# Pooled attention feeding a GELU MLP: first batch by two head pairs at a time, v over two queues, weight loads in longer runs, one multiply moved ahead of an eviction

## The chip, the cores and the metric

The kernel runs on one core of a Trainium2 chip. The metric is the device time in microseconds (us) of one execution; smaller is better. Five engines work side by side, each with its own list of instructions that it takes in order: TensorE (PE; its weight loads are shown as PEld), VectorE (DVE), ScalarE (ACT), GpSimd (POOL) and SyncE (SP). SP, ACT and POOL also issue DMA transfers, and the profile numbers the queues behind them: q1 belongs to SP, q10 to ACT, q0 to POOL.

## What is computed

q, k and v are f32, 8 batches x 8 heads x 576 positions x 64. k and v are averaged over groups of 8 positions, so that each head has 72 keys. Attention follows, its result is laid out as 4608 rows of 512, and an MLP with a tanh GELU takes it to the output.

```python
k_p = k.reshape(B, H, 72, 8, D).mean(axis=3)
v_p = v.reshape(B, H, 72, 8, D).mean(axis=3)
attn = softmax(scale * q @ k_p^T)            # 8 x 8 x 576 x 72
x = (attn @ v_p).transpose(0, 2, 1, 3).reshape(4608, 512)
out = gelu_tanh(x @ w_in) @ w_out            # 512 -> 2048 -> 512
```

## The kernel before, in words

**Two interleaved pipelines.** Attention goes batch by batch (8 batches of 576 rows), the MLP group by group (`NG` = 9 groups of 512 rows). Attention fills `xT`, the transposed input of the MLP, column by column. While group g is in its second multiplication (`p2_mm`, L290), the attention of batch g+1 is woven into it by hand: `todo` (L397 to L428) says ahead of which of the 64 second-multiplication matmuls each step of the attention stands. The schedule is manual: each engine executes its instructions in the order in which the program writes them down, and waits are put in by the framework where data or buffers ask for it.

**Attention of a batch.** For each of 8 items (c, pr), c being a half of the queries and pr a pair of heads: `qk` (L208) makes two score matmuls into two PSUM banks, `expo` (L216) takes the exponential on ACT, `av` (L224) multiplies with v and with ones (which gives the softmax's denominators), `norm` (L241) takes Ln and Exp(-x) on ACT, which is the reciprocal, and `mult` (L252) multiplies on DVE into `xT`. k and v are pooled by DVE additions (`k_steps` L147, `v_steps` L154). `trans_k` (L168) transposes pooled k on PE and copies it into `kTs`, even rows for c = 0 and odd rows for c = 1; `trans_q` (L184) transposes q in four pieces `QG`, two of queries with heads 0 to 3 and two with heads 4 to 7.

**An MLP group.** `p1_mm` (L280): for each of 16 chunks fo of 128 hidden units, 4 matmuls over ko = 0..3 (128 rows of the input each), 512 columns. `gelu` (L285) evicts the chunk on ACT. Then 4 x 16 matmuls of `p2_mm`, and `store` (L294), a DVE eviction and four output DMAs for each 128 rows. Chunk ko of the first multiplication reads what head pair ko of the attention gave.

**The start, batch 0 (L95 to L140 and L305 to L348).** SP and ACT load k, SP loads v in two halves of four heads; each half comes as two DMAs, partitions 0 to 63 and 64 to 71. POOL loads q in two halves, then, in the order of its queue: the first two quarters of w_in, k and q of batch 1, the other two quarters of w_in, four quarters of w_out. PE runs `spin` matmuls (L309), which nobody reads, to stay busy. All 8 score items come first, then the 8 items' `av`, `norm` and `mult` one after the other. After the fourth `mult`, a small memset of the v buffer (L344) releases SP to load v of batch 1. The first 16 first-multiplication matmuls on the 288 columns of c = 0 are put among the last items; the other 224 columns follow.

**Group 0 (L351 on).** Beside its chunks fo stand, by `plan` (L372), the preparation of batch 1: k additions at fo 0, k transpose at 4, four q transposes at 6 to 9, v additions at 10 and 12. Its second multiplication runs in blocks of four fo over two output banks, so that it starts on the first quarter of w_out alone.

**At each change of group** (L404 to L415), the last item's multiply comes after the 64th matmul, and the seventh item's too (position 55 + 9 = 64), so that DVE takes the last eviction of the group ahead of both. The first matmuls of the next group follow at once on PE; those with ko = 2 and 3 read what the seventh and eighth multiply write.

Of the kernel before, what the change touches and what calls it, by code (L numbers as in the profile page):

```python
# [18 lines left out]
def kernel(  # L19
# [45 lines left out]
    def load_k(b, engs):  # L65
        rows = k[b].rearrange("h (j l) d -> (h j) (l d)", l=8)
        main = rows[0:128 * KR].rearrange("(p r) c -> p r c", r=KR)
        n = KR // len(engs)
        for i, eng in enumerate(engs):
            eng.dma_start(out=kts[b % 2][:, i * n:(i + 1) * n], in_=main[:, i * n:(i + 1) * n])  # L70
        engs[-1].dma_start(out=kts[b % 2][64:128, KR], in_=rows[128 * KR:])

    def load_v(b, eng, h0=0, h1=H):
        if b not in vs:
            vs[b] = kvp.tile([Sp, H, 512], F32, name="vt")
        rows = v[b, h0:h1].rearrange("h (j l) d -> j h (l d)", l=8)

        for j0, j1 in ((0, 64), (64, Sp)) if eng is nc.sync else ((0, Sp),):
            eng.dma_start(out=vs[b][j0:j1, h0:h1], in_=rows[j0:j1])
# [8 lines left out]
    w_in_b = consts.tile([128, KO, DF], BF16, name="w_in_b")  # L88
    w_out_b = consts.tile([128, FO, DM], BF16, name="w_out_b")
    w_in_v = moe_w_in.rearrange("(ko p) f -> p ko f", p=128)  # L90
    w_out_v = moe_w_out.rearrange("(fo p) d -> p fo d", p=128)
# [4 lines left out]
    load_v(0, nc.sync, 0, 4)  # L96
    load_v(0, nc.sync, 4, 8)
# [4 lines left out]
    def load_w_in(i):  # L102
        nc.gpsimd.dma_start(out=w_in_b[:, :, i * 512:(i + 1) * 512], in_=w_in_v[:, :, i * 512:(i + 1) * 512])  # L103

    load_w_in(0)
    load_w_in(1)
# [4 lines left out]
    kTs = [consts.tile([128, 2, H, Sp], BF16, name=f"kT{i}") for i in range(2)]  # L111
# [11 lines left out]
    nc.vector.memset(kTs[0], 0.0)  # L123
# [4 lines left out]
    nc.gpsimd.memset(kTs[1], 0.0)  # L128
    nc.gpsimd.memset(kps[1], 0.0)
    nc.gpsimd.memset(kts[1][0:64, KR], 0.0)  # L130
    nc.gpsimd.memset(vps[0], 8.0)  # L131
    nc.gpsimd.memset(vps[1], 8.0)  # L132

    load_k(1, [nc.gpsimd])
    load_q(1)
    load_w_in(2)
    load_w_in(3)
    for i in range(4):
        nc.gpsimd.dma_start(out=w_out_b[:, 4 * i:4 * i + 4, :], in_=w_out_v[:, 4 * i:4 * i + 4, :])

# [27 lines left out]
    def trans_k(b, bank, odd_eng=None):  # L168
        tp = half_bank(bank)[:, 0:(KR + 1) * 128].rearrange("p (r c) -> p r c", c=128)
        kf = kps[b % 2].rearrange("p r d -> p (r d)")  # L170
        for r in range(KR + 1):
            nc.tensor.transpose(out=tp[:, r, :], in_=kf[:, r * D:r * D + 128], identity=identb)  # L172
        tp = tp[0:D]
        n7 = (H - 1) * KH
        for e in range(2):
            copy = nc.scalar.copy if e and odd_eng is nc.scalar else nc.vector.tensor_copy
            o = kTs[b % 2][e * 64:(e + 1) * 64, e]
            copy(out=o[:, 0:H - 1].rearrange("p h (j r) -> p h j r", r=KR),  # L178
                 in_=tp[:, 0:KR, 0:n7].rearrange("p r (h j) -> p h j r", j=KH))
            copy(out=o[:, H - 1, 0:(128 - n7) * KR].rearrange("p (j r) -> p j r", r=KR),  # L180
                 in_=tp[:, 0:KR, n7:128].rearrange("p r j -> p j r"))
            copy(out=o[:, H - 1, (128 - n7) * KR:], in_=tp[:, KR, 64:128])

    def trans_q(b, i, t0, n, bank, eng):  # L184
        if b not in qTs:
            qTs[b] = bp.tile([128, 2, TP, 128], BF16, name="qT")
        tp = half_bank(bank)[:, 0:n * 128].rearrange("p (t c) -> p t c", c=128)
        for x in range(n):
            nc.tensor.transpose(out=half_bank(bank)[:, x * 128:(x + 1) * 128],
                                in_=qs[b][:, i, (t0 + x) * 128:(t0 + x + 1) * 128],  # L190
                                identity=identb)
        o = qTs[b][:, i, t0:t0 + n]
        if eng is nc.scalar:
            nc.scalar.copy(out=o, in_=tp)
        else:
            nc.vector.tensor_copy(out=o, in_=tp)

# [10 lines left out]
    def qk(b, c, pr, bank):  # L208
        for e in range(2):
            h = 2 * pr + e  # L210
            nc.tensor.matmul(out=PS[:Sp, bank + e, :CH].rearrange("j (t p) -> j t p", p=32),  # L211
                             lhsT=kTs[b % 2][:, c, h, :],
                             rhs=qTs[b][:, h // 4, :, h % 4 * 32:h % 4 * 32 + 32],
                             start=True, stop=True)
# [26 lines left out]
    def norm(b, c, pr, bank):  # L241
        ld = ep.tile([128, CH], F32, name="ld")
        if b:
            nc.scalar.activation(out=ld[0:64], in_=PS[64:128, bank, :CH], func=ACT.Ln)  # L244
            nc.scalar.activation(out=ld[64:128], in_=PS[0:64, bank + 1, :CH], func=ACT.Ln)  # L245
        else:
            nc.scalar.activation(out=ld, in_=PS[:, bank + 1, :CH], func=ACT.Ln)
        rc = ep.tile([128, CH], F32, name="rc")
        nc.scalar.activation(out=rc, in_=ld, func=ACT.Exp, scale=-1.0)  # L249
        rcs[b, c, pr] = rc  # L250

    def mult(b, c, pr, bank):  # L252
        rc = rcs.pop((b, c, pr))
        col = b * S + c * CH
        for x in range(2 if b else 1):
            rows = slice(x * 64, (x + 1) * 64) if b else slice(0, 128)
            nc.vector.tensor_tensor(out=xT[rows, pr, col:col + CH], in0=PS[rows, bank + x, :CH],  # L257
                                    in1=rc[rows], op=ALU.mult)

# [9 lines left out]
    def h_bank(g, fo):  # L269
        x, y = x_bank(g), 1 - x_bank(g)  # L270
        if fo == 4:
            return 7
        return (x, 2, 3, y)[fo if fo < 4 else (fo - 1) % 4]
# [6 lines left out]
    def p1_mm(g, fo, ko, c0=0, c1=GROUP):  # L280
        r0 = g * GROUP
        nc.tensor.matmul(out=PS[:, h_bank(g, fo), c0:c1], lhsT=w_in_b[:, ko, fo * 128:(fo + 1) * 128],  # L282
                         rhs=xT[:, ko, r0 + c0:r0 + c1], start=(ko == 0), stop=(ko == KO - 1))
# [20 lines left out]

    act_set(EXP_SET)  # L305
    for s in k_steps(0):
        s()

    def spin(n):  # L309

        for _ in range(n):
            nc.tensor.matmul(out=PS[:, 7, :], lhsT=idle[:, 0:128], rhs=idle, start=True, stop=True)  # L312

    def scores(b, c, pr, bank):
        qk(b, c, pr, bank)
        expo(b, c, pr, bank)

    spin(16)
    trans_q(0, *QG[0], 5, nc.scalar)
    trans_q(0, *QG[1], 6, nc.scalar)  # L320
    spin(4)
    trans_k(0, 4, nc.scalar)
    trans_q(0, *QG[2], 5, nc.vector)
    trans_q(0, *QG[3], 6, nc.vector)
    spin(2)
    for i, (c, pr) in enumerate(((0, 0), (0, 1), (1, 0), (1, 1), (0, 2), (0, 3), (1, 2), (1, 3))):
        if i:
            spin(1)
        scores(0, c, pr, (2, 0)[i % 2])
    for hf in range(2):  # L330
        for s in v_steps(0, hf):
            s()

    early = [(fo, ko) for ko in range(KO) for fo in range(4)]
    take = (0, 0, 0, 0, 0, 4, 6, 6)
    for i, (c, pr) in enumerate(ORDER):
        bank = (4, 6, 0, 2, 4, 6, 4, 6)[i]
        av(0, c, pr, bank)
        norm(0, c, pr, bank)
        mult(0, c, pr, bank)  # L340
        if i == 3:

            vs[1] = kvp.tile([Sp, H, 512], F32, name="vt")
            nc.vector.memset(vs[1][:, 0, 0:1], 0.0)  # L344
            load_v(1, nc.sync)
        for fo, ko in early[:take[i]]:
            p1_mm(0, fo, ko, 0, CH)
        early = early[take[i]:]  # L348


    for g in range(NG):  # L351
        nb = g + 1 if g + 1 < B else None
        act_set(GELU_SET)
        if g + 2 < B:

            load_q(g + 2)
            trans_q_dma(g + 2)
            nc.gpsimd.tensor_copy(out=gate, in_=qTs[g + 2][0:1, 1, TP - 1, 0:2])  # L358
            load_k(g + 2, [nc.gpsimd])
            load_v(g + 2, nc.gpsimd)  # L360


        side = {fo: [] for fo in range(FO)}
        if nb is not None:
            kk = k_steps(nb)
            v0, v1 = v_steps(nb, 0), v_steps(nb, 1)
            tk = [lambda: trans_k(nb, 4)]
            if g:
                plan = {2: kk[:1], 3: kk[1:], 7: v0[:1], 8: v0[1:], 9: tk, 11: v1[:1], 12: v1[1:]}
            else:  # L370
                tq = [lambda a=a, i=i: trans_q(nb, *a, 4 + i, nc.vector) for i, a in enumerate(QG)]
                plan = {0: kk, 4: tk, 6: tq[:1], 7: tq[1:2], 8: tq[2:3], 9: tq[3:], 10: v0, 12: v1}  # L372
# [5 lines left out]
        if g == 0:  # L378
            first = [(fo, ko, CH) for ko in range(KO) for fo in range(4)]
        else:  # L380
            late = 3
            rest = [fo for fo in range(4) if fo != late]
            first = [(fo, ko, 0) for ko in range(2) for fo in rest]
            first += [(late, 0, 0), (late, 1, 0)]
            first += [(fo, ko, 0) for ko in (2, 3) for fo in rest + [late]]
        for fo, ko, c0 in first:
            p1_mm(g, fo, ko, c0)
        for fo in range(FO):
# [4 lines left out]
            for s in side[fo]:  # L393
                s()

# [6 lines left out]
        if nb is not None:  # L402
            act_set(EXP_SET)
            pos = (6, 14, 20, 27, 34, 41, 48, 55, 61)  # L404
            for i in range(len(ORDER) + 1):
# [7 lines left out]
                if i:  # L413
                    at(pos[i], norm, *a)
                    at(min(pos[i] + 9, 65), mult, *a)  # L415
# [43 lines left out]
```

The softmax here doesn't subtract the row's maximum and nothing guards it: scores larger than these inputs give would overflow.

## Time and profile before

| what | value |
|---|---|
| device time, median of 3 runs | 311.97 us (310.83 to 312.3) |
| device time of the profiled execution | 311.66 us |
| its span, first to last instruction | 309.9 us |
| granted TensorE clock, mean | 0.999 |
| PE busy | 296.7 us (96%) |
| ACT busy | 220.9 us (71%) |
| DVE busy | 157.1 us (51%) |
| L282 and L291, the MLP's matmuls, of 128x512 | 548 and 560 in the trace, 379 ns each |
| weight loads of L282 (128 columns) | 98 ns each |
| read from HBM, written | 36.70 MB, 9.44 MB |

Spans of PE overlap, since matmuls are pipelined: the 379 ns of a matmul are its latency, and a dense run of them starts one about every 216 ns. So 16 of them make a row of 3.63 us in the timeline (15 starts and one latency). Times within the execution are counted from the start of the span. A bracket at the end of a line of the timeline tells how long the engine had been idle and what ended that. In the view of DMAs by stretch, a share is the time that packets of a queue took, as part of 16 engines' time; shares add up to over 100% where packets overlap.

### The profile page before, as it was taken

How to read it: one execution, taken by the hardware profiler on the slowest of the kernel's cores; microseconds unless marked ns; L12 is line 12 of the kernel's file. 1: busy time of each engine (PE TensorE's matmuls, PEld its weight loads, DVE VectorE, ACT ScalarE, POOL GpSimd, SP SyncE). 2: the span in 40 equal slices, each digit the busy share in tenths (PEclk: the TensorE clock that was granted, in tenths of full speed). 3: DMA queues.
4: the chain of work that ended last, by engine and by line, in shares of the span. 5: the costliest groups of instructions: out<-in, count | busy, mean ns of one | idle time of the engine just before them, and what ended most of it. 6: DMA issues, size and time to landing. Idle time of an engine off the chain costs nothing.

```text
span 309.9 us, 4249 instructions
## 1 busy us (share of the span) xinstructions
PE 296.7 (96%) x1516; PEld 149.5 (48%) x1545; DVE 157.1 (51%) x304; ACT 220.9 (71%) x414; POOL 30.8 (10%) x54
## 2 busy tenths in 40 slices
PE   7788899999999999999999999999999999999994
PEld 2455455444544455445544554455445544444441
DVE  3867536647568455855495358636772640020011
ACT  1597478877997799778987898689868987306500
POOL 8530000300301200030003000200000000000000
PEclk9999999999999999999999999999999999999999
DMA  7999995894895982588358826572101120121022
GB/s 225 232 279 249 178 200 116 266 225 87 258 224 113 237 186 62 112 225 175 85 110 232 185 68 100 166 182 68 41 0 33 49 56 0 36 68 34 2 68 69
DMA packets 32701, 41.05 MB, mean 132 GB/s; under 512 B 17608, under 2 KB 21704, under 8 KB 31784
## 3 DMA queue, kind: packets, MB, share of 16 engines
q0 software_dynamic: 10160, 24.26, 35.4%
q1 hardware_dynamic: 22200, 15.74, 21.8%
q10 hardware_dynamic: 320, 0.79, 0.8%
q8 instruction: 12, 0.20, 0.3%
q14 instruction: 9, 0.07, 0.1%
HBM read 36.70 MB, written 9.44 MB: 149 GB/s over the span
## 4 chain that ended last, share of the span: by engine, by line
PE 83%; DMA 12%; POOL 2%; issue 1%; ACT 0%; DVE 0%; POOLq 0%
PE PS L291 38%; PE PS L282 36%; DMA w_out_b<-in_moe_w_out_dram 8%; DMA kt<-in_k_dram 4%; PE PS L211 4%; PE PS L231 4%; PE PS L172 1%; POOL w_in_b L103 0%; POOL kT L128 0%; POOL qb L84 0%; POOL vp L131 0%; POOL vp L132 0%; DVE osb L296 0%; ACT e L218 0%; POOL kt L130 0%
## 5 line engine op out<-in xcount | busy, mean ns | idle before, releaser
L291 PE MATMUL PS<-w_out_b,gT 128*128 128x512 bf16 x560 | 133.8, 379 | 0.9
L282 PE MATMUL PS<-xT,w_in_b 128*128 128x512 bf16 (+2 forms) x580 | 128.3, 373 | 1.8 <-DMA w_in_b<-in_moe_w_in_dram 0.9
L288 ACT ACTIVATE gT<-PS 128x512 bf16<-128x512 f32 x144 | 81.3, 603 | 48.4 <-PE PS L282 48.2
L282 PEld LDWEIGHTS <-w_in_b 128*128 128x128 bf16 x592 | 57.2, 98 | 66.4 <-issue 2.0
L291 PEld LDWEIGHTS <-gT 128*128 128x128 bf16 x576 | 56.0, 97 | 57.1 <-issue 0.8
L296 DVE COPY osb<-PS 128x512 f32<-128x512 f32 x36 | 24.9, 692 | 94.9 <-PE PS L291 94.9
L257 DVE TENSOR_TENSOR xT<-PS,rc 64x288 bf16<-64x288 f32 (+1 forms) x120 | 54.6, 455 | 29.9 <-ACT rc L249 22.3
L218 ACT ACTIVATE e<-PS 72x576 bf16<-72x576 f32 x64 | 40.7, 644 | 8.4 <-PE PS L211 7.6
L145 DVE TENSOR_TENSOR vt<-vt 72x1024 f32<-72x1024 f32 (+1 forms) x32 | 30.5, 952 | 7.0 <-DMA vt<-in_v_dram 6.2
L249 ACT ACTIVATE rc<-ld 128x288 f32<-128x288 f32 x64 | 28.3, 443 | 2.1
L211 PE MATMUL PS<-qT,kT 128*72 128x288 bf16 x128 | 26.1, 286 | 0.4 <-ACT e L218 0.3
L244 ACT ACTIVATE ld<-PS 64x288 f32<-64x288 f32 x56 | 22.8, 408 | 1.4
L245 ACT ACTIVATE ld<-PS 64x288 f32<-64x288 f32 x56 | 22.5, 402 | 1.4
L263 ACT ACT_TABLE_LOAD x17 | 21.8, 1283 | 2.1 <-issue 1.8
L231 PE MATMUL PS<-e,vp 72*128 72x288 bf16 x112 | 23.1, 285 | 0.0
L211 PEld LDWEIGHTS <-kT 128*72 128x72 bf16 x128 | 14.4, 113 | 14.2 <-issue 1.4
L145 DVE TENSOR_TENSOR kt<-kt 128x1280 f32<-128x1280 f32 (+1 forms) x16 | 18.5, 1158 | 4.7 <-DMA kt<-in_k_dram 4.3
L358 POOL COPY gate<-qT 1x2 bf16<-1x2 bf16 x6 | 1.1, 176 | 155.8 <-DMA qT<-qb 155.8
L178 DVE COPY kT<-PS 64x504 bf16<-64x504 bf16 x15 | 10.1, 675 | 7.1 <-PE PS L172 7.0
L231 PEld LDWEIGHTS <-vp 72*128 72x128 bf16 x112 | 11.0, 98 | 3.3
L312 PE MATMUL PS<-idle 128*128 128x512 bf16 x28 | 9.6, 467 | 1.2 <-DVE idle L120 1.2
L145 DVE TENSOR_TENSOR vp<-vt 72x128 bf16<-72x128 f32 x28 | 6.9, 284 | 0.6
(45 smaller groups left out, 75.5 us busy)
## 6 DMA issues: line engine op xcount, KB each, us to landing
out_dram<-osb SPq DMA_DIRECT2D x142, 64.0 KB, 1.7
kt<-in_k_dram POOLq DMA_DIRECT2D x7, 1024.0 KB, 5.8
vt<-in_v_dram POOLq DMA_DIRECT2D x6, 1152.0 KB, 12.4
qb<-in_q_dram POOLq DMA_DIRECT2D x7, 576.0 KB, 15.1
w_in_b<-in_moe_w_in_dram POOLq DMA_DIRECT2D x4, 512.0 KB, 18.4
w_out_b<-in_moe_w_out_dram POOLq DMA_DIRECT2D x4, 512.0 KB, 25.0
vt<-in_v_dram SPq DMA_DIRECT2D x2, 512.0 KB, 11.1
vt<-in_v_dram SPq DMA_DIRECT2D x1, 1024.0 KB, 11.6
```

What stands on the lines that cost most here:

```text
L145: nc.vector.tensor_tensor(out=o, in0=a, in1=b, op=ALU.add)
L211: nc.tensor.matmul(out=PS[:Sp, bank + e, :CH].rearrange("j (t p) -> j t p", p=32), lhsT=kTs[b % 2][:, c, h, :], rhs=qTs[b][:, h // 4, :, h ...
L218: nc.scalar.activation(out=e, in_=PS[:Sp, bank:bank + 2, :CH], func=ACT.Exp, scale=1.0 / 64.0)
L231: nc.tensor.matmul(out=PS[:, bank + x, :CH], lhsT=flat(vps[b % 2][:, pr, x]), rhs=e[:, x, :], start=True, stop=True)
L244: nc.scalar.activation(out=ld[0:64], in_=PS[64:128, bank, :CH], func=ACT.Ln)
L245: nc.scalar.activation(out=ld[64:128], in_=PS[0:64, bank + 1, :CH], func=ACT.Ln)
L249: nc.scalar.activation(out=rc, in_=ld, func=ACT.Exp, scale=-1.0)
L257: nc.vector.tensor_tensor(out=xT[rows, pr, col:col + CH], in0=PS[rows, bank + x, :CH], in1=rc[rows], op=ALU.mult)
L282: nc.tensor.matmul(out=PS[:, h_bank(g, fo), c0:c1], lhsT=w_in_b[:, ko, fo * 128:(fo + 1) * 128], rhs=xT[:, ko, r0 + c0:r0 + c1], start=(ko ...
L288: nc.scalar.activation(out=gTs[g][:, fo, :], in_=PS[:, h_bank(g, fo), :], func=ACT.Gelu_apprx_tanh)
L291: nc.tensor.matmul(out=PS[:, o_bank(g, r), :], lhsT=gTs[g][:, fo, r * 128:(r + 1) * 128], rhs=w_out_b[:, fo, :], start=(fo == 0), stop=(fo ...
L296: nc.vector.tensor_copy(out=osb, in_=PS[:, o_bank(g, r), :])
```

## The change

- **Loads.** v of batch 0: the first half on SP, the second on ACT, no longer both on SP. The last piece of k moves from ACT to SP. w_in comes as two halves of 1024 columns (4 KB runs of f32) in two tiles, no longer four quarters (2 KB runs). w_out's rows are dealt to partitions in fours, so that each of its four DMAs reads 8 KB runs. For that the hidden units of a chunk are taken with a step of four: the weight load of `p1_mm` reads every fourth column. POOL's queue is now q (two), first half of w_in, k of batch 1 (ahead of most of its memsets), second half of w_in, q of batch 1, w_out.
- **Batch 0.** Pooled k first in the transposes; all copies of transposed k on DVE. The first v addition stands on DVE ahead of the two copies of transposed q for heads 4 to 7. `av`, `norm` and `mult` go by two head pairs: one Ln, one Exp and one multiply of 128 x 2 x 288. The order is pairs 0 and 1 for c = 0, then c = 1, then pairs 2 and 3. The last three DVE additions of v's second half stand after the first multiply. Spins fill the waits (22 at the start, then 6, 5, 2 and 3); they write into banks of the attention, so they wait for the multiplies that read those.
- **Group 0's first 16 matmuls** are of 512 columns into banks 4 to 7, after the last spins. v of batch 1 is released by the memset after the third (of four) multiplies.
- **Plan of group 0.** k transposes at fo 6, q transposes at 10 to 13, v additions at 13 and 14. Loads for batch 2 are written after the chunks, not ahead of them.
- **Every batch.** `kTs` is two tiles; the seventh multiply stands at position 62 at the latest, ahead of the last eviction, no longer after it.

```diff
-        engs[-1].dma_start(out=kts[b % 2][64:128, KR], in_=rows[128 * KR:])
+        engs[0].dma_start(out=kts[b % 2][64:128, KR], in_=rows[128 * KR:])
...
+    HALVES = [((0, 64, h, h + 4), (64, Sp, h, h + 4)) for h in (0, 4)]
+    WHOLE = ((0, 64, 0, H), (64, Sp, 0, H))
...
-    w_out_v = moe_w_out.rearrange("(fo p) d -> p fo d", p=128)
+    w_out_v = moe_w_out.rearrange("(q p j) d -> p q (j d)", p=128, j=4)
...
-    load_v(0, nc.sync, 0, 4)
-    load_v(0, nc.sync, 4, 8)
+    load_v(0, nc.sync, HALVES[0])
+    load_v(0, nc.scalar, HALVES[1])
...
-        nc.gpsimd.dma_start(out=w_in_b[:, :, i * 512:(i + 1) * 512], in_=w_in_v[:, :, i * 512:(i + 1) * 512])
+        nc.gpsimd.dma_start(out=w_in_b[i], in_=w_in_v[:, :, i * 1024:(i + 1) * 1024])
...
+    def norm0(c, pr, bank):
+        ld = ep.tile([128, 2, CH], F32, name="ld0", bufs=1)
+        nc.scalar.activation(out=ld, in_=PS[:, bank + 1:bank + 4:2, :CH], func=ACT.Ln)
+        rc = ep.tile([128, 2, CH], F32, name="rc0")
+        nc.scalar.activation(out=rc, in_=ld, func=ACT.Exp, scale=-1.0)
+        nc.vector.tensor_tensor(out=xT[:, pr:pr + 2, c * CH:(c + 1) * CH], in0=PS[:, bank:bank + 3:2, :CH],
+                                in1=rc, op=ALU.mult)
...
-        nc.tensor.matmul(out=PS[:, h_bank(g, fo), c0:c1], lhsT=w_in_b[:, ko, fo * 128:(fo + 1) * 128],
+        q, j = divmod(fo % 8, 4)
+        nc.tensor.matmul(out=PS[:, h_bank(g, fo), c0:c1], lhsT=w_in_b[fo // 8][:, ko, q * 512 + j:(q + 1) * 512:4],
...
+    spin(22, 1)
+    t = kts[0]
+    for r in (slice(0, KR), slice(KR, KR + 1)):
+        add(t[:, r, 0:256], t[:, r, 0:256], t[:, r, 256:512])
+    for s in k_steps(0)[1:]:
+        s()
+    nc.gpsimd.memset(kps[1], 0.0)
+    nc.gpsimd.memset(kts[1][0:64, KR], 0.0)
+    load_k(1, [nc.gpsimd])
+    load_w_in(1)
+    load_q(1)
...
+    trans_k(0, 4)
+    trans_q(0, *QG[0], 5, nc.scalar)
+    trans_q(0, *QG[1], 6, nc.scalar)
+    scores(0, 0, 2)
+    scores(0, 1, 0)
+    va[0]()
+    trans_q(0, *QG[2], 5, nc.vector)
+    trans_q(0, *QG[3], 6, nc.vector)
+    for i, (c, pr) in enumerate(((1, 0), (1, 1), (0, 2), (0, 3), (1, 2), (1, 3))):
+        spin(1, 7)
+        scores(c, pr, (2, 0)[i % 2])
+    for s in va[1:] + vb[:1]:
+        s()
...
+    early = [(fo, ko) for ko in range(2) for fo in range(4)]
+    av0(0, 0, 4)
+    norm0(0, 0, 4)
+    for s in vb[1:]:
+        s()
+    av0(1, 0, 0)
+    norm0(1, 0, 0)
+    spin(5, 5)
+    av0(0, 2, 4)
+    norm0(0, 2, 4)
+    vs[1] = kvp.tile([Sp, H, 512], F32, name="vt")
+    nc.vector.memset(vs[1][:, 0, 0:1], 0.0)
+    load_v(1, nc.sync, WHOLE)
+    spin(2, 1)
+    av0(1, 2, 0)
+    norm0(1, 2, 0)
+    spin(3, 5)
+    for fo, ko in early:
+        p1_mm(0, fo, ko)
...
-                plan = {0: kk, 4: tk, 6: tq[:1], 7: tq[1:2], 8: tq[2:3], 9: tq[3:], 10: v0, 12: v1}
+                plan = {0: kk, 6: tk, 10: tq[:1], 11: tq[1:2], 12: tq[2:3], 13: tq[3:] + v0, 14: v1}
...
-                    at(min(pos[i] + 9, 65), mult, *a)
+                    at(min(pos[i] + 9, 62 if i < len(ORDER) else 65), mult, *a)
```

## The prediction

> **What bounds the kernel now.** I read the page's slices first, then a table of busy time by stage, then the timeline of the first 60 us.
>
> ```profile
> PE   7788899999999999999999999999999999999994
> PEclk9999999999999999999999999999999999999999
> ```
>
> ```profile
> 0.00:12.46 12.46, 8.47 (x45) 3.86 (x46) 6.35 (x15) 3.21 (x6) 11.07 (x21) 1.00 0.89 233
> 12.46:16.67 4.21, 3.94 (x24) 2.45 (x24) 2.87 (x7) 3.76 (x7) 0.05 (x1) 1.00 1.38 201
> 16.67:25.65 8.98, 7.90 (x66) 6.03 (x64) 6.60 (x14) 8.17 (x19) 2.92 (x4) 1.00 1.13 277
> 25.65:40.03 14.38, 12.29 (x72) 5.92 (x72) 9.69 (x20) 8.52 (x15) 0.00 (x0) 1.00 1.28 211
> 40.03:58.33 18.30, 18.05 (x96) 9.58 (x97) 7.95 (x17) 15.95 (x32) 2.94 (x5) 1.00 0.83 163
> 58.33:90.45 32.12, 31.94 (x164) 16.11 (x166) 19.34 (x37) 26.62 (x51) 2.92 (x5) 1.00 0.81 215
> ```
>
> After each stretch stand its length, the busy time of PE, PEld, DVE, ACT and POOL, the granted clock, the DMA share and GB/s. From 58.33 on PE is full (31.94 of 32.12 us) at the full clock, and the change adds no PE work there. So it is decided ahead of 58.33, where group 0's second multiplication ends. From the first score matmul (12.46) to there are 45.87 us; the work in it, at one start per 0.216 us for 512 columns, 0.122 for 288 and 0.056 for 128, is 128 x 0.216 + 80 x 0.122 + 23 x 0.056 = 38.7. These 7 us of waits and spins, and part of the 12.46, are all there is to win. Up to 40 us the DMA engines are full too (shares of about 1).
>
> **Part 1: to the first scores.** k's additions start at 7.25, with its last piece. Split, its main part (in by 6.4) goes first: 1024 elements 1.22 us (the 72x1024 row), 256 elements about 0.42 (on the line through 0.69 for 512 and 1.22 for 1024), then 0.83 and 0.49. Pooled k is ready at 9.4, not 10.13. The scores also wait for ACT's two copies of transposed q (0.69 and 0.59): they start at 11.55 and the exponentials at 12.0, **0.9 earlier**.
>
> **Part 2: v over two queues.** How queues share is in the DMA view from 6.5 to 10 us:
>
> ```profile
> q0 software_dynamic: 237, 0.47, 70.0%
> q1 hardware_dynamic: 235, 0.46, 38.6%
> ```
>
> Packets, MB, share. The two take turns packet by packet (237 to 235), though one of q takes 0.165 us (70% of 16 x 3.5 us, by 237) and one of v 0.092. With three queues a turn is 2 x 0.092 + 0.165 = 0.35 us, 46 packets per us and queue. When k's main part is through (landed at 6.0, so 5.3 or a little earlier), SP has k's last 64 packets and 288 of v ahead of it: 7.7 us, and about 1 us to land: v's first half is in at **14.0**. Before, DVE took it at 12.82 without waiting for it. The second half, on ACT, comes at about 13 and not at 16.5:
>
> ```profile
> 12.82 1.93 DVE L145 TENSOR_TENSOR vt<-vt 72x1024 f32<-72x1024 f32 x2
> ...
> 16.54 1.94 DVE L145 TENSOR_TENSOR vt<-vt 72x1024 f32<-72x1024 f32 x2 [1.27 <-DMA vt<-in_v_dram]
> 18.52 0.49 DVE L145 TENSOR_TENSOR vz<-vt 72x128 bf16<-72x128 f32 x2
> ```
>
> Bounds for the first half: 11.7, if k, q and v alone fill the engines (256 x 0.149 + 640 x 0.092 + 256 x 0.165 = 139, 8.7 us by 16, from 2 us on and 1 us to land; 0.149 is half the 0.298 of part 4), and 14.6, if the 8-partition piece goes slowly at the end. I take 14.0.
>
> Behind that addition stand, on DVE, the copies of transposed q for heads 4 to 7; for them waits the fifth score item, and on PE, in order, everything after it. Addition 1.22, copies 0.49 and 0.42: 16.2. The fifth exponential starts 0.45 later (as 12.46 to 12.91 before), at 16.65; four at 0.575 end at 19.0. Before, the eight ended at 17.5. So part 1's gain becomes a **loss of 1.5**.
>
> **Part 3: norm by two pairs.** ACT: Ln of 288 takes 0.395, Exp 0.443; with 0.93 ns per further element (0.395 to GELU's 0.603 at 512) 576 take 0.66 and 0.71, less 0.06 overlap: 1.3 per two pairs, where two single ones took 1.55 (0.775 apart). That saves 1.0 in all. But fewer, longer links chain PE, ACT and DVE: av of two pairs 8 x 0.122 = 0.98 (18.0 to 19.0), 0.2 lag, 1.3 on ACT (20.5), multiply 0.76 (21.3; 0.455 for 288 plus 288 x 1.04 ns), then v's second half 0.69 + 0.49 (22.5), for which the third av waits; 0.98, 0.2, 1.3 and 0.8 more end the third multiply at 25.9. The spins after it wait for its banks: 3 x 0.216, and the first MLP matmul starts at **26.5**. The fourth multiply is done at 27.2, ahead of ko = 2 (28.2). From there PE is dense: 64 x 0.216 + 23 x 0.056 = 15.1, second multiplication from 41.6 (before: 40.03), 1.6 late.
>
> **Part 4: longer runs.** From 36 to 46 us 1851 packets of 1 KB (2 KB read) go by, 0.086 us each per engine; from 18.5 to 20 us 8 KB packets:
>
> ```profile
> q0 software_dynamic: 78, 0.61, 96.7%
> ```
>
> 16 x 1.5 x 0.967 / 78 = 0.298 us for four times the bytes, against 0.346. w_out gains 2048 x 0.086 / 16 - 512 x 0.298 / 16 = 1.5 us of DMA time. Both weight waits go (before: PE idled 0.68 at 32.0 and 0.59 at 36.6 for w_in, and 0.3 at 46.7 for w_out). The first two are in part 3's dense 15.1; the third makes the second multiplication 18.0 and not 18.3: it ends at 59.6, **1.3 late**.
>
> **Part 5: v of batch 1.** Its memset now follows the third multiply of two pairs: issue at 26.0, not 21.23. Before:
>
> ```profile
> 35.52 1.94 DVE L145 TENSOR_TENSOR vt<-vt 72x1024 f32<-72x1024 f32 x2 [0.58 <-DMA vt<-in_v_dram]
> ```
>
> 14.3 us from issue to DVE: none of its packets until 25.1 (the DMA view of 21.3 to 25.1 has q0 alone), 512 packets in turns with w_in's 1 KB packets until 31.9, and the 64 of the last 8 partitions. Now its neighbours on q0 are w_out's packets of 8 KB read. By turns, 512 x (0.298 + 0.092) / 16 = 12.5 and not 6.8: 26.0 + 14.3 + 5.7 = 46.0. Pooling its first half takes 1.22 + 0.69 + 0.49: ready at 48.4. The first av of batch 1 stands 14 matmuls and 4 score matmuls into the second multiplication, at 41.6 + 3.5 = 45.1, and all of PE is behind it: **3.3 us**. The other bound is 0: if the queues shared by time, 512 packets would take about 6 us as before, and 40.3 + 2.4 is early enough. I take the turns, since the row of 6.5 to 10 us, with packets of unequal length, is the nearest.
>
> The Trainium skill's page "TensorE: Matmul & The Clock Gate", section "What's actually happening", says that a TensorE idle for a free-running window of about 3.4 us falls to half clock. Here PE idled 2.0 us at 6.9 and PEclk stayed at 9; a wait of 3.3 us would be at the edge, and falling over it would by that page add an estimated 1.7 us (one window at half speed).
>
> **Part 6: the seventh multiply.** In groups 1 to 3 the first 21 matmuls take 4.96 us (58.33 on), against 20 x 0.216 + 0.379 = 4.70 dense: 0.26 lost, since DVE takes the eviction (58.53, 0.69) and both multiplies (to 61.1) in that order. Moved up, the seventh ends 0.7 sooner, the eighth as late as before less what DVE idled. I take 3 x 0.17 = **0.5 gained** of 0.8 possible; later groups do not read those columns.
>
> **Costs I put at nothing.** Weight loads with a step of four: 98 ns each, hidden under 216 ns of matmul. No row has such a load. From below nothing; from above, if the 128 columns took four times as long, 392 ns, 0.18 us in each of 576 matmuls, 101 us. Of 98 ns some is fixed, so twice (196) would still hide. I take 0. The Trainium skill's page "SBUF — State Buffer", section "Door 1: The DMA port swizzle", holds that bf16 may be read at steps up to 8 elements at full rate, which would make it 0 as well; no run here shows it. Memsets on POOL move behind loads; POOL is idle from 24 to 54 us. Batch 2's loads follow w_out, which lands earlier.
>
> **Sum.** + 1.3 + 3.3 - 0.5 = + 4.1: 311.66 (the profiled execution: span 309.9 and 1.76 around it) becomes **315.8**. The median of the three runs, 311.97, is 0.3 higher, inside the range.
>
> **Rivals.**
> - *v of batch 1 comes in time* (sharing by time, or an earlier start): 311.66 + 1.3 - 0.5 = 312.5. For it: 14.3 us of latency are partly unexplained. Against: the turns.
> - *Not slower: v of batch 0 is early.* If its first half lands by 12.3, addition and copies end at 14.4, the exponentials go on almost unbroken and end at 17.2; each later step is 1.8 earlier, less what DVE's second half takes: first MLP matmul at 24.7, and without the later wait the second multiplication ends at 24.7 + 15.1 + 18.0 = 57.8. With 0.5 to 0.8 from part 6: 310.5 to 310.2. It decides from a landing of about 13.0 on. Against: the packets' turns.
> - *Strided weight loads are not hidden.* Each ns over 216 costs 0.58 us (576 matmuls): 250 ns would add 20 and give 335.4. The load's busy row would show it.
>
> **How the numbers follow.** The forecast 0.55, the first rival 0.22, the second 0.18, the third 0.05. Half a per cent, 1.6 us, is about what a measurement here tells from no change. Slower: 0.50 of the forecast and the third, 0.55; faster: most of the second, 0.15; same: the rest, 0.30. The range goes from the second rival's 310.2 to the forecast with a stall 1.2 longer, 317.0 (v's first half at 14.6, and the last 64 packets of the other v in turns with q's, 8 per engine at 0.165).
>
> **What would show it.** Right: DVE's fifth-item copies wait for v (14 us), first MLP matmul near 26.5, and DVE waiting for v of batch 1 until about 46 while PE idles near 45. Wrong: v of batch 0 in by 12.5, or v of batch 1 before 42; then parts 2 or 5 fail. The weight load of L293 at 98 ns confirms the cost put at nothing.

## The result, and the profile after

The changed kernel takes **319.39 us** (median of 4 runs, 318.87 to 320.1); the kernel before, on the same chip, 311.71 (310.83 to 312.3). The ratio is 1.025, 95% interval [1.0217, 1.0284]. The change costs 7.7 us, nearly twice the 4.1 of the forecast, and the time is above its range. The profiled execution takes 320.1 us with a span of 318.3, so 8.4 more than the 309.9 of before. First its slices, PE busy and the granted clock:

```profile
PE   8679999999999999999999999999999999999994
PEclk9875999999999999999999999999999999999998
```

A slice is 8 us. In the second to fourth slice, from 8 to 32 us, the clock is at 8, 7 and 5 tenths, where before it was 9 throughout. In the fourth slice PE looks *fuller* than before (9 against 8), because at half clock the same matmuls take twice as long. The table by stage, with the boundaries of before (length, busy time of PE, PEld, DVE, ACT, POOL, clock, DMA share, GB/s):

```profile
0.00:12.46 12.46, 8.86 (x40) 3.90 (x40) 7.03 (x19) 3.02 (x5) 10.02 (x21) 1.00 0.89 240
12.46:16.67 4.21, 3.38 (x16) 1.98 (x16) 0.55 (x1) 1.92 (x4) 0.54 (x1) 0.59 1.34 180
16.67:25.65 8.98, 7.13 (x30) 4.12 (x31) 5.32 (x11) 4.87 (x8) 1.24 (x2) 0.66 1.09 274
25.65:40.03 14.38, 14.38 (x62) 7.39 (x61) 5.52 (x9) 7.82 (x13) 0.00 (x0) 0.74 1.07 227
40.03:58.33 18.30, 18.29 (x106) 10.06 (x105) 10.90 (x24) 13.44 (x24) 2.91 (x5) 1.00 0.71 181
```

Busy time alone would mislead: 16.67 to 25.65 shows PE busy for 7.13 us, but with 30 matmuls where before had 66 in 7.90 us. The clock column (0.59, 0.66, 0.74) tells why. The trace's own clock record has full clock from 5.96, half from 12.79 to 16.20, full to 19.62, half to 33.27: 17.06 us at half, always in whole windows of 3.41 us.

DVE's timeline around v of batch 0, then of batch 1:

```profile
16.12 1.22 DVE L136 TENSOR_TENSOR vt<-vt 72x1024 f32<-72x1024 f32 x1 [4.47 <-DMA vt<-in_v_dram]
17.27 0.81 DVE L194 COPY qT<-PS 128x640 bf16<-128x640 bf16 x2
...
47.44 1.94 DVE L136 TENSOR_TENSOR vt<-vt 72x1024 f32<-72x1024 f32 x2 [0.33 <-DMA vt<-in_v_dram]
```

DVE can take v's first half only at 16.12 (before at 12.82), and the copies of transposed q stand behind it. v of batch 1 comes at 47.44, but PE does not wait for it: the second multiplication starts only at 48.14, and the first product with that v stands at 51.65. PE's timeline:

```profile
18.13 0.44 PE L213 MATMUL PS<-qT,kT 128*72 128x288 bf16 x2 [1.97 <-DVE qT L194]
...
24.75 2.29 PE L319 MATMUL PS<-idle 128*128 128x512 bf16 x5 [0.33 <-DVE xT L265]
26.83 0.69 PE L238 MATMUL PS<-e,ones 72*128 72x288 bf16 x2
...
66.16 4.03 PE L293 MATMUL PS<-xT,w_in_b 128*128 128x512 bf16 x17
```

The pair of 288 columns takes 0.69 us here and 0.41 at full clock; five spins take 2.29 and not 1.24. The first MLP matmul is at 32.80 (forecast 26.5), group 1 starts at 66.16, 7.83 later than before (58.33). From there to the end of the span it is 252.14 us, before 251.53. So 7.83 + 0.61 = 8.44 is all of the difference, and each kernel below can be read by the same marks. The marks are those of the profiled execution; its time is given where it lies more than 0.5 us from the median:

| kernel | median, us | second multiplication from | group 1 from | from there to the end |
|---|---|---|---|---|
| before | 311.5 to 311.7 | 40.03 | 58.33 | 251.5 |
| after | 319.39 | 48.14 (in an execution of 320.1) | 66.16 | 252.1 |
| e1: spins | 318.06 | 44.09 (in one of 317.11) | 63.23 | 252.1 |
| e2: v on one queue | 317.30 | 40.83 | 63.62 | 252.1 |
| e3: both | 316.31 | 41.50 | 61.95 | 252.1 |
| e10: e1, v of batch 1 early | 316.13 | 44.21 | 62.23 | 252.1 |
| e6: e3, v of batch 1 early | 311.94 | 40.04 | 58.05 | 252.1 |
| e8: e6, seventh multiply back | 311.41 | 41.71 (in one of 313.13) | 59.73 | 251.6 |
| e9: e8, waits filled | 310.56 | 38.93 | 56.95 | 251.5 |
| e4: before, multiply early | 311.86 | 38.98 | 57.57 | 252.1 |
| e5: before, longer runs | 312.86 | 42.32 (in one of 313.65) | 60.34 | 251.5 |
| e7: before, warm-up spins on 72 rows | 312.01 (one execution) | 40.43 | 58.60 | 251.6 |
| e11: before, no spins inside | 314.10 | 42.77 | 60.78 | 251.6 |

### The profile page after: what moved, and what is told of

Its sections match the earlier page's. It is cut to its first block, busy times and chain, and to the rows that moved or that the text cites. A ratio compares the mean times of both kernels' runs of the same rounds, so it can differ in the third digit from the quotient of the medians.

```text
span 318.3 us, 4258 instructions
## 1 busy us (share of the span) xinstructions
PE 307.5 (97%) x1538; PEld 161.2 (51%) x1538; DVE 157.4 (49%) x305; ACT 219.6 (69%) x403; POOL 28.5 (9%) x53
## 3 DMA queue, kind: packets, MB, share of 16 engines
q1 hardware_dynamic: 21968, 15.28, 19.9%
## 4 chain that ended last, share of the span: by engine, by line
PE 92%; DMA 4%; DVE 1%; ACT 1%; issue 1%; SPq 1%; DVEq 0%
PE PS L293 39%; PE PS L302 39%; PE PS L213 5%; PE PS L233 4%; DMA vt<-in_v_dram 4%; PE PS L238 2%; PE PS L319 2%; PE PS L163 1%; PE PS L182 0%; DVE qT L194 0%; DVE xT L265 0%; DVE osb L307 0%; ACT rc L264 0%; ACT ld L262 0%; ACT e L220 0%
## 5 line engine op out<-in xcount | busy, mean ns | idle before, releaser
L302 PE MATMUL PS<-w_out_b,gT 128*128 128x512 bf16 x576 | 136.2, 379 | 0.0
L293 PE MATMUL PS<-xT,w_in_b 128*128 128x512 bf16 x576 | 128.9, 379 | 0.2
L293 PEld LDWEIGHTS <-w_in_b 128*128 128x128 bf16 x576 | 64.7, 113 | 58.8 <-issue 2.9
L256 DVE TENSOR_TENSOR xT<-PS,rc 64x288 bf16<-64x288 f32 x112 | 51.0, 455 | 31.2 <-ACT rc L248 28.9
L213 PE MATMUL PS<-qT,kT 128*72 128x288 bf16 x128 | 26.8, 294 | 3.1 <-DVE qT L194 2.0
L248 ACT ACTIVATE rc<-ld 128x288 f32<-128x288 f32 x56 | 24.8, 443 | 1.8
L136 DVE TENSOR_TENSOR kt<-kt 128x640 f32<-128x640 f32 (+3 forms) x17 | 18.7, 1100 | 3.4 <-DMA kt<-in_k_dram 2.9
L169 DVE COPY kT<-PS 64x504 bf16<-64x504 bf16 x16 | 10.8, 675 | 13.3 <-PE PS L163 13.2
L319 PE MATMUL PS<-idle 128*128 128x512 bf16 x38 | 15.3, 544 | 1.5 <-DVE idle L123 1.2
L319 PEld LDWEIGHTS <-idle 128*128 128x128 bf16 x38 | 4.9, 131 | 7.6 <-issue 4.8
```

The lines of the kernel that those rows point to most:

```text
L136: nc.vector.tensor_tensor(out=o, in0=a, in1=b, op=ALU.add)
L302: nc.tensor.matmul(out=PS[:, o_bank(g, r), :], lhsT=gTs[g][:, fo, r * 128:(r + 1) * 128], rhs=w_out_b[:, fo, :], start=(fo == 0), stop=(fo ...
L319: nc.tensor.matmul(out=PS[:, bank, :], lhsT=idle[:, 0:128], rhs=idle, start=True, stop=True)
```

## Experiments

**The clock or the transfer: e1, e2, e3.** Theory C: the interior spins that the change took out (4 and 2, around the transposes) covered PE's waits; without them, and with v late, the clock falls. Rival: v of batch 0 alone makes the loss. e1 puts spins back, e2 puts v of batch 0 on one queue again (and k's last piece on ACT), e3 does both.

```diff
+    spin(4, 7)
     scores(0, 0, 2)
     scores(0, 1, 0)
+    spin(3, 7)
     va[0]()
...
-        spin(1, 7)
+        spin(9 if i == 2 else 1, 7)      (e3: 2 if i == 2)
```

```diff
-    load_v(0, nc.scalar, HALVES[1])
+    load_v(0, nc.sync, HALVES[1])
```

> The changed kernel with idle matmuls put back into three waits of PE ahead of v (4 after the first q transposes, 3 after the first two score items, 9 and not 1 where the fifth item waits for DVE). Theory C (clock: the change took the idle matmuls out of the first scores, and two windows of 3.4 us in which PE was busy about 37% let the granted clock fall to half for 17.1 us): the clock stays at 1.0 throughout, the first MLP matmul comes at about 28.3 us and not at 32.8, time about 314.6. What is left over 311.7 is then the wait for v, the longer chain by two pairs, and the order of the seventh multiply. Theory Q (the late v of batch 0 is the whole cause, and the clock only follows it): v is as late as before, so the time stays near 319; it gains at most 1 us.

> The changed kernel with v of batch 0 on SP alone and k's last piece on ACT, as in the kernel before; no other idle matmuls. Theory Q: v's first half is in by 11.8, DVE does not wait for it, the second fall of the clock (19.6 to 33.3) does not come, time about 313. Theory C: the first fall (12.8) comes all the same, since the waits ahead of it do not hang on v; whether a second follows depends on how busy PE is afterwards: 313 without, 317 with.

> Both: v of batch 0 on SP alone, and idle matmuls (4, 3 and 2) in the waits. Both theories: clock 1.0 throughout, exponentials unbroken, first MLP matmul about 24.7, second multiplication of group 0 ends at 57.8, time about 311.7, the same as the kernel before. If it is later, the chain by two pairs (fewer and longer links between PE, ACT and DVE) costs more than the 1 us that it saves on ACT.

e1: ratio 1.020 [1.0174, 1.0227]. In the profiled execution the clock stays full, and the first MLP matmul comes at 29.00, 3.80 earlier, although DVE has v 0.37 later (16.49). So the clock is worth about 4 us of that stage; yet the median falls by only 1.3, not by the expected 5. The profiled execution, the fastest of four, is 3.0 below that of after; two of the others have a mean granted clock of 0.989 and 0.995, so the spins did not hold the clock in all four. e2: 1.0172 [1.0143, 1.02]; the second multiplication starts at 40.83, 7.3 earlier, and the time falls by 2.1. The first fall of the clock comes all the same (10.95 to 14.36), as theory C had it, and the long one from 19.62 does not. Where the rest went stands in e2's timeline of DVE and PE:

```profile
44.96 1.94 DVE L136 TENSOR_TENSOR vt<-vt 72x1024 f32<-72x1024 f32 x2 [5.17 <-DMA vt<-in_v_dram]
47.01 0.49 DVE L136 TENSOR_TENSOR vp<-vt 72x128 bf16<-72x128 f32 x2
...
47.36 0.50 PE L233 MATMUL PS<-e,vp 72*128 72x288 bf16 x2 [2.85 <-DVE vp L136]
```

This is the wait for v of batch 1, almost as part 5 forecast it (3.3 us near 45). After it the clock falls for another window (48.50 to 51.91). In e1 the wait is 0.87, in e3 2.18; there the clock falls only from 19.52 to 22.93. But e3, which both theories put at about 311.7, takes 316.31 (ratio 1.0155 [1.0127, 1.0184]). Neither theory alone holds: three losses lie behind one another, and taking one away uncovers the next.

**v of batch 1 early: e6, e10.** The memset that releases this load goes from behind the third multiply to behind the last v addition of batch 0. e6 does it to e3, e10 to e1.

```diff
     for s in vb[1:]:
         s()
+    vs[1] = kvp.tile([Sp, H, 512], F32, name="vt")
+    nc.vector.memset(vs[1][:, 0, 0:1], 0.0)
+    load_v(1, nc.sync, WHOLE)
```

> As e3 (spins put back, v of batch 0 on one queue), and v of batch 1 released after the last v addition of batch 0 (about 20.7 us) and not after the third multiply. Theory C (the clock, then the wait for v of batch 1, then the late start of the dense part): v reaches DVE before 41, the 2.35 us wait ahead of the first attention product of batch 1 goes, w_out comes 3 us later and is still in time; 316.31 - 2.35 = about 314.0 us. Rival Q (v of batch 1 only takes its turn from w_in's second half and w_out, which then come late): v still after 43, or a wait for w_in or w_out of over 1 us in the dense part: 315.3 or more.

> As e1 (the kernel after with spins put back, v of batch 0 over two queues), and v of batch 1 released after the last v addition of batch 0. It prices the two queues for v by itself against e6, from which it differs in nothing else. Theory C: the clock stays at 1.0, the wait for v of batch 1 goes, the first MLP matmul stays at about 29 and the second multiplication at 44: 4 us later than in e6, so 315.5 to 316.2 us. Rival: the two queues cost nothing once the clock and v of batch 1 are put right: 312 to 313 us.

e6: 1.0028 [1.0008, 1.0048], 311.94, 2 us better than expected. v of batch 1 reaches DVE at 39.51 (issue 20.9), and no product waits:

```profile
39.51 1.95 DVE L136 TENSOR_TENSOR vt<-vt 72x1024 f32<-72x1024 f32 x2 [0.51 <-DMA vt<-in_v_dram]
41.56 0.49 DVE L136 TENSOR_TENSOR vp<-vt 72x128 bf16<-72x128 f32 x2
...
43.55 0.41 PE L233 MATMUL PS<-e,vp 72*128 72x288 bf16 x2
```

Between the profiled executions of e3 and e6 lie 3.9 us: 2.4 from the second multiplication to group 1, and 1.5 ahead of it, where e3 has a half-clock window and e6 none. That window is not the edit's doing alone: e8 below is the same as e6 up to there, and its profiled execution has one. e10: 316.13, 1.0179 [1.013, 1.0229], as theory C expected (315.5 to 316.2), with full clock in batch 0 and no such wait in the profiled execution (one of four, at 319.43, has a mean clock of 0.982). It differs from e6 in the queues of v of batch 0, and also in k's last piece (SP, not ACT) and in nine spins, not two, ahead of the fifth score product. These two do not make the difference: the first score product stands at 11.49 (e6: 11.47), and the nine spins end before the product can start:

```profile
14.94 2.11 PE L319 MATMUL PS<-idle 128*128 128x512 bf16 x9
18.61 0.44 PE L213 MATMUL PS<-qT,kT 128*72 128x288 bf16 x2 [1.57 <-DVE qT L194]
```

So the two queues cost 4.2 us here. The fifth score product is at 18.61 (e6: 14.47), behind v's addition at 16.60 (e6: 12.16).

**The seventh multiply: e4, e8.** e4 is the kernel before with that one edit, e8 is e6 without it.

```diff
-                    at(min(pos[i] + 9, 65), mult, *a)
+                    at(min(pos[i] + 9, 62 if i < len(ORDER) else 65), mult, *a)
```

> The kernel before with the seventh multiply at position 62, nothing else. The trace of the changed kernel shows 0.19 us lost between the sixth and seventh first-multiplication matmul of each of 7 groups (PE waits for the last eviction, now behind the multiply), where the kernel before lost 0.26 in 3 groups: plus 0.6 us, 312.3. The prediction's part 6 said minus 0.5: 311.2.

> As e6, and the seventh multiply at position 64 again, after the last eviction. Theory C: the 0.57 us that groups 1 to 8 took longer goes: 0.5 to 0.6 below e6, about 313.4 us, and what is left against the kernel before is the second multiplication of group 0 starting about 1.5 us later. Rival: the position is worth nothing here, within 0.2 of e6.

e4: 311.86 against 311.46, ratio 1.001 [0.9997, 1.0023], by itself not decisive. But every kernel with the edit takes 252.1 us from group 1 on and every kernel without it 251.5 or 251.6, and e8 is 0.53 below e6, as expected (ratios 1.0009 [0.9992, 1.0026] and 1.0028). In after each of the seven changes of group has 0.19 us more than the usual 0.216 from the start of the sixth MLP matmul to that of the seventh, which waits for the last eviction; before, three changes had 0.26 (7 x 0.19 - 3 x 0.26 = 0.55). e8's executions fall in two groups: eight at 311.2 to 311.6, two at 313.0 and 313.1. All are below the 313.4 expected, since e6 already was. The profiled one is of the second, with one half-clock window (19.96 to 23.38).

**Longer runs alone: e5.** The kernel before, with w_in in two halves, w_out dealt in fours and the strided weight loads.

```diff
-        nc.gpsimd.dma_start(out=w_in_b[:, :, i * 512:(i + 1) * 512], in_=w_in_v[:, :, i * 512:(i + 1) * 512])
+        nc.gpsimd.dma_start(out=w_in_b[i], in_=w_in_v[:, :, i * 1024:(i + 1) * 1024])
```

> The kernel before with the longer weight runs alone (w_in in two halves, the second half where its third quarter stood; w_out dealt in fours; strided weight loads). Theory R (longer runs save what part 4 of the prediction said): the waits for w_in (0.68 and 0.59 at 32 and 36.6) and for w_out (0.3 at 46.7) go, weight loads of 113 ns stay hidden, v of batch 1, still issued at 21, reaches DVE before 41: 310.2 to 310.8 us. Rival S (strided loads or turns with longer packets cost what the runs save): within 0.3 us of the kernel before, or slower, and then a wait on the pooled v of batch 1 or gaps between dense matmuls above 0.216 us show it.

312.86, ratio 1.0057 [1.0039, 1.0076]: slower, as rival S has it, but through v of batch 0 and not of batch 1. DMA view from 12 to 13 us, packets, MB and share, of before and then of e5:

```profile
q1 hardware_dynamic: 81, 0.17, 62.9%
q0 software_dynamic: 84, 0.09, 50.4%
```

```profile
q0 software_dynamic: 65, 0.13, 69.9%
q1 hardware_dynamic: 66, 0.14, 39.6%
```

Both give equal turns, but with w_in's longer packets a turn is longer: v of batch 0 on q1 moves 66 packets and not 81. Its second half reaches DVE at 17.72, before at 16.54, and PE idles 2.18 us ahead of the third product. In the profiled execution (313.65) the clock falls for two windows, 19.54 to 26.37.

**What the clock counts: e7, e11.** e7 is the kernel before with its 16 warm-up spins on 72 rows of the array, e11 the kernel before without the 13 spins inside batch 0. Neither changes what is computed.

> The kernel before with its 16 warm-up matmuls on 72 rows of the array and not 128; everything else as it was. Theory W (the clock gate weighs activity by the rows in use): after the warm-up the granted clock stays at half, and goes to 1.0 one or more windows of 3.41 us later than 5.5 us. Rival T (only the time that TensorE is busy counts): the clock goes to 1.0 at about 5.5 us as before, and 62 percent of half-clock windows need another reason.

> The kernel before without its 13 spins inside batch 0 (4, 2 and seven single ones); the 16 at the start stay. Nothing that is computed changes. Theory C (these spins are what keeps the clock up): one or two half-clock windows between 8.9 and 20 us, and 1 to 3 us more. Rival: the attention's own matmuls keep the clock up and the spins only delay: 311.5 us or less, clock 1.0 throughout.

PE's timeline of e7:

```profile
1.21 7.01 PE L312 MATMUL PS<-idle 72*128 72x512 bf16 x16 [1.21 <-DVE idle L120]
```

In e7 PE is busy without a gap for 7.01 us, and the record stays at half until 13.90 (before: 5.46): theory W. It costs little (312.01, in one execution): the first score product is 1.31 us later than before, the second multiplication only 0.40. e11: 314.10 (312.7 to 314.18), ratio 1.0067 [1.0037, 1.0097]. Without the spins the clock is at half from 10.07 to 27.13, five windows where one or two were expected; its slices:

```profile
PEclk9657999999999999999999999999999999999998
```

I then counted, in all thirteen traces, the share of each clock window of the first 36 us in which matmuls run (a matmul of 512 columns counts 0.216 us at full and 0.43 at half clock), once as it is and once weighted by its rows of 128:

| kernel, window | clock in it | share | by rows | clock after it |
|---|---|---|---|---|
| after, 9.38 to 12.79 | full | 0.37 | 0.37 | half |
| after, 16.20 to 19.62 | full | 0.36 | 0.36 | half |
| e3, 16.11 to 19.52 | full | 0.61 | 0.36 | half |
| e8, 16.55 to 19.96 | full | 0.58 | 0.35 | half |
| before, 5.46 to 8.88 | full | 0.38 | 0.38 | full |
| before, 15.70 to 19.12 | full | 0.62 | 0.45 | full |
| e7, 3.66 to 7.07 | half | 1.00 | 0.56 | half |
| after, 26.44 to 29.86 | half | 1.00 | 0.72 | half |
| e8, 19.96 to 23.38 | half | 1.00 | 0.78 | full |
| after, 29.86 to 33.27 | half | 1.00 | 0.79 | full |

The share by rows separates all windows: at full clock the seven with 0.37 or less fell and all from 0.38 on stayed; at half the eleven up to 0.72 stayed and the twenty from 0.78 on rose. The plain share does not (0.61 fell, 0.38 stayed; 1.00 stayed at half, 0.82 rose). The weighting was formed on the trace of after and then tested by e7; the two bounds are fitted to these traces. At full clock they lie so close (0.374 fell, 0.378 stayed) that the exact bound is not shown: some matmul records can be missing, and counting lengths a little differently makes the two equal. Weighting by the columns of the weights as well does not separate the windows (at half clock 0.64 rose, e2 from 10.95, and 0.72 stayed); other weightings were not run.

**A version below both: e9.** e8, with the three waits left in batch 0 taken on: the piece of 8 partitions of v's second half goes over ACT's queue, all additions of v stand ahead of the first multiply, and the last spins are short ones into columns that nobody reads, so that they wait for no multiply.

```diff
-    load_v(0, nc.sync, HALVES[1])
+    load_v(0, nc.sync, HALVES[1][:1])
+    load_v(0, nc.scalar, HALVES[1][1:])
...
+            nc.tensor.matmul(out=PS[:, 7, CH:512], lhsT=idle[:, 0:128], rhs=idle[:, CH:512], start=True, stop=True)
...
-    spin(5, 5)
+    fill(12)
```

> As e8, with the three waits of batch 0 that were left taken on: the piece of 8 partitions of v's second half goes over ACT's queue (it landed 1.9 us after the piece of 64), all additions of v stand ahead of the first multiply, and the spins 5, 2 and 3, which waited for a multiply's bank, become 12, 3 and 9 short ones of 224 columns into columns that nobody reads. Theory C (what is left after the undoing is the late second half of v and half-clock windows): third attention product at 19.8 and not 20.9, first MLP matmul at about 23.3 and not 24.9, no half-clock window in any run, 309.5 to 310.3 us, below the kernel before. Rival: the chain of norms on ACT sets the end, or the new waits are elsewhere (v of batch 1, transposes): 311 us or more.

310.56 (310.27 to 311.87, 12 runs) against 311.58, ratio 0.9978 [0.9962, 0.9995]: 1 us below the kernel before, 8.8 below the changed one, and a little above the 309.5 to 310.3 expected.

```profile
16.18 1.94 DVE L137 TENSOR_TENSOR vt<-vt 72x1024 f32<-72x1024 f32 x2 [0.71 <-DMA vt<-in_v_dram]
...
18.35 1.31 PE L324 MATMUL PS<-idle 128*128 128x224 bf16 x12
19.78 0.41 PE L239 MATMUL PS<-e,ones 72*128 72x288 bf16 x2
...
23.84 3.40 PE L294 MATMUL PS<-xT,w_in_b 128*128 128x512 bf16 x15
```

v's second half is there at 16.18 (e6: 17.79), the third product starts at 19.78 (20.86), the first MLP matmul at 23.84 (24.94; expected 23.3). Three of its twelve runs lie 1.2 us above the others (311.66 to 311.87), so "no half-clock window in any run" is not shown; the profiled execution has none.

## Why the prediction was wrong

The sign was right, and several steps held; what failed is that it carried **the granted clock through batch 0 as 1.0**. Step by step:

- *Part 1, first scores at 11.55, exponentials at 12.0:* 11.46 and 11.90. Held.
- *Part 2, turns packet by packet:* held closely. From 6.5 to 10 us the three queues of after move

```profile
q0 software_dynamic: 157, 0.32, 49.5%
q10 hardware_dynamic: 155, 0.32, 30.4%
q1 hardware_dynamic: 156, 0.30, 28.4%
```

  and the piece of 64 partitions of v's first half lands at 14.13 (forecast 14.0). But the addition needs the piece of 8 partitions too, and this landed at 16.0, 1.9 later, past the bound of 14.6. The fifth exponential starts at 18.61, not 16.65: the term is 2.0 too small. (In e6, on one queue, the last pieces come 1.0 and 1.9 after the large ones, in the kernel before 0.5 and 1.4.)
- *Part 3, first MLP matmul at 26.5, second multiplication at 41.6:* 32.80 and 48.14, 6.3 and 6.5 late. 2.0 is v's; 3.80 is the clock, by e1, or 4.2 if one allows for e1's fifth exponential, which is 0.36 later with its v; so 0.1 to 0.5 stays open. This is the step that failed. Its chain of norms counted av of two pairs as 8 x 0.122, right only at full clock. Where batch 0 was forecast to wait longer, no price was put on PE idling while it waits. The spins were counted with the waits, as time to be won; in the kernel before they were what held the clock (e11). The clock was weighed once, for the wait near 45.
- *Part 4:* the second multiplication takes 18.02, not 18.30, as forecast; the w_in waits are gone as well. But the gain is given back before: e5 shows that the longer packets make v of batch 0 1.2 us later. Landing of w_out moved from 39.1 to 32.9 for its first quarter.
- *Part 5, v of batch 1 at 46.0 on DVE, a wait of 3.3 us:* issued at 31.25 and not 26.0, and on DVE at 47.44, with no wait, as PE was later still. In e2, whose second multiplication starts at 40.83, the forecast is nearly met: 44.96 and a wait of 2.85; from issue (25.08) to DVE it takes 19.9 us, forecast 20.0. And the queues took turns there by packet, not by time, as e2's view of 32 to 36 us shows:

```profile
q0 software_dynamic: 173, 0.64, 79.2%
q1 hardware_dynamic: 175, 0.36, 25.9%
```

  So the mechanism was right, and hidden by the late start of the second multiplication.
- *The skill's rule there.* The Trainium skill, "TensorE: Matmul & The Clock Gate", section "What's actually happening", has the clock fall after an idle window of about 3.4 us. The windows of 3.41 us agree, and so does the price (e8's two groups lie 1.7 us apart, the estimate of 1.7). But no window here was idle where the clock fell: matmuls filled 0.23 to 0.61 of it.
- *Part 6, 0.5 gained:* 0.61 lost. The seventh multiply ahead of the last eviction makes the next group's seventh matmul wait for the bank of that eviction, at all seven changes; I had counted only the three where the old order lost something. Wrong sign.
- *Strided weight loads at nothing:* they cost 113 ns against 98 (114 in e5) and stay hidden; dense matmuls still start every 0.216 us. The skill's page "SBUF — State Buffer", section "Door 1: The DMA port swizzle", has steps up to 8 elements at full rate; the trace shows 15% more, which here costs nothing.

- *Two sums are 0.1 off:* the terms of the chain in part 3 end the third multiply at 25.8, not 25.9, and those of the second rival give 310.6 to 310.3, not 310.5 to 310.2. Neither matters here.

In one line: forecast +1.3 (batch 0) +3.3 -0.5; measured +7.83 (beyond the 1.3, 2.0 are v and 3.8 or more the clock), 0, +0.61. Undone one after the other, by the medians, the four causes are: clock and v of batch 1 together 3.3 (after to e10), the two queues 4.2 (e10 to e6), the seventh multiply 0.5 (e6 to e8). What is left of the change in e8, norm by two pairs, longer runs and new plan, together with the spins and the early load that were put in, is worth nothing that can be told from zero.

## What to carry to other kernels

Before taking out a spin, or making a wait longer, count what TensorE does in each 3.4 us around it, weighted by the rows its matmuls use; a late transfer costs a second time when the clock falls during the wait. Causes that lie behind one another cannot be priced by undoing one: here one repair gave 1.3 us, another 2.1, and all four 8. A transfer is as late as its last piece, and it takes turns with whatever packets its neighbours have, so longer packets for one load delay another.

## What the runs showed of the hardware

- The granted clock follows matmuls weighted by their rows, in these traces: spins on 72 rows, dense for 7 us, did not raise it (e7), and a window filled to 0.61, much of it with products on 72 rows, let it fall (e3).
- Three queues whose packets kept the engines for unequal times (49.5, 30.4 and 28.4%) still moved 157, 155 and 156 packets.
- The same kernel can run with or without a half-clock window near the bounds: in e8 311.2 to 311.6 or 313.0 to 313.1.
- A transfer of 32 packets over 8 partitions, behind one of 256 over 64 on the same queue, landed 0.5 to 1.9 us after it (before, e6, and v's first half in after); moved to ACT's queue it was out of the way (e9).
